# A fused attention, gated MLP and mixer kernel: four edits where its stages meet

## The chip, the core and the metric

The kernel runs on one core of one Trainium2 chip. The metric is the device time of one execution in microseconds; three runs of the kernel before took 915.26, 916.33 and 917.14 us, median 916.33.

## What is computed

Three layers in a row, for 4 batches of 448 tokens and 768 channels (12 heads of 64):

```
scores = q @ k.T / sqrt(64) - log(448);  x = sigmoid(scores) @ v           # attention
xk, xr = mu * x + (1 - mu) * x_prev                                        # mix with the token before
x = sigmoid(xr @ w_r) * (relu(xk @ w_k) ** 2 @ w_v)                        # gated MLP
h = relu(x.T @ w_tok1) @ w_tok2;   u = x + h.T                             # token mixing
out = u + relu(u @ w_ch1) @ w_ch2                                          # channel mixing
```

## The kernel before

Two batches lie beside one another as 896 columns, channels on partitions, so `rows` holds six rows of 128 channels by 896 columns. All stages run once for batches 0 and 1 and again for 2 and 3: `attention`, `first_part` (gated MLP and token mixing), `second_part` (channel mixing).

The large products keep about 22 bits of each operand: weight and activation are split into a high half (rounded to fp32r by ACT) and a low half (what is left, subtracted by DVE). `products` (line 293) multiplies high by high, high by low and low by high, for each tile of 128 in the sum, 512 and 384 columns wide one after the other (`WIDE`), so a channel product is 6 x 3 x 2 = 36 matmuls. The weights come as 8-byte numbers and are made into fp32 by the kernel: `w_raw` loads one on SP's queue, `w_form` takes two passes of ACT (lines 195, 196), `w_join` two of DVE (199, 202), `w_high` rounds on ACT (240), `w_low` subtracts on DVE (244). `raws`, formed weights and halves have three buffers each.

The order of work is written out by hand: each engine runs its instructions in the order of the program. `weights()` hands out the halves of the next weight and puts the steps for later weights into the list `due`; `products` takes one step from it (`tick`) after each tile of its sum, so the preparation of weights lies between matmuls. Four PSUM buffers of two banks go round (`new_ps`).

The places that matter:

- Start: the first loads of k and q go out on SP (lines 117, 118); twelve idle matmuls (`WARM`, line 132) run on zeros; then come the first scores (160), of 64 rows for each of two heads, evicted by a sigmoid on ACT (169).
- End of the gated MLP: line 382 multiplies a row by the product. Its rows are transposed for token mixing by `y_transpose` (319), whose result is evicted in two pieces: ACT 321, DVE 322 for three quarters, then ACT 323, DVE 324 for the tail.
- Token mixing, first product (lines 392 to 405): three pieces of two rows each, two halves `j` of eleven matmuls per piece. Row 5 is transposed after piece 0, `j` 0; only piece 2 reads it. All due steps of the first weight are run ahead of the pieces; those of the second lie in the second product.
- Token mixing, second product (lines 408 to 417): six rows `m`. A row takes 12 matmuls of 448 columns; then DVE adds it to `rows` (415), ACT rounds it to u's high half (416), DVE subtracts for the low half (417).
- Channel mixing: the first products read u row by row in the sum. The last products are added to `rows` (434) and written out as two transfers, one per batch, on SP (437).

Of the kernel before, what the change touches and what calls it, by code (L numbers as in the profile page):

```python
# [14 lines left out]
ALU = mybir.AluOpType  # L15
PSUM = bass.MemoryType.PSUM

B, H, S, D = 4, 12, 448, 64
# [4 lines left out]
P = 128  # L23
NT = C // P
# [2 lines left out]
W = 2 * S  # L27

WIDE = ((0, 512), (512, W - 512))
WARM = 12  # L30


def f32(ap):
    return ap.bitcast(F32)
# [3 lines left out]
def kernel(  # L38
# [17 lines left out]
    PE, ACT, DVE, POOL, SP = nc.tensor, nc.scalar, nc.vector, nc.gpsimd, nc.sync  # L56

    def pool(name, bufs, **kw):
        return ctx.enter_context(tc.tile_pool(name=name, bufs=bufs, **kw))

    const = pool("const", 1)
    wraw, wpool, wsplit = pool("wraw", 3), pool("wpool", 3), pool("wsplit", 3)
    tmps = pool("tmps", 2)
    psum = pool("psum", 4, space=PSUM)

# [10 lines left out]
    rows = const.tile([P, NT, W], F32, tag="rows", name="rows")  # L76
# [21 lines left out]
    def beside(ap):  # L98
        return ap.rearrange("p (b n) -> p b n", b=2)

    heads = [const.tile([P, 2 * 4 * P + S], F32, tag="qkv%d" % i, name="qkv") for i in range(3)]
    kns = [t[:, : 4 * P] for t in heads]
# [3 lines left out]
    def new_ps():  # L106
        return psum.tile([P, 1024], F32, tag="ps", name="ps")
# [7 lines left out]
    def load_kq(i):  # L115
        b, pr = units[i]
        SP.dma_start(out=kns[i % 3], in_=k[b * NPAIR + pr])
        SP.dma_start(out=qns[i % 3], in_=q[b * NPAIR + pr])

    def load_v(i):  # L120
        b, pr = units[i]
        SP.dma_start(out=vns[i % 3], in_=v[b * NPAIR + pr])

    warm = const.tile([P, 1], F32, tag="warm", name="warm")
    DVE.memset(warm, 0.0)
    ACT.activation(warm, warm, AF.Sigmoid)
# [4 lines left out]
    for _ in range(WARM):  # L131
        PE.matmul(idle[:, :S], zero[:, :P], zero, start=True, stop=True)  # L132

    load_kq(0)
    load_v(0)
    load_kq(1)
    load_v(1)
# [69 lines left out]
    for w in (w_r, w_k, w_v, w_tok1):  # L207
        n, r, cols = w.shape
# [14 lines left out]
    def w_raw(upto):  # L223
        for i, r, kt in step("raw", upto):
            raws[i] = wraw.tile([P, NT, P, 2], U32, tag="raw", name="raw")[:r, :kt]
            SP.dma_start(out=raws[i].rearrange("p t n e -> p (t n e)"), in_=seq[i][0])

    def w_form(upto):
        for i, r, kt in step("form", upto):
            forms[i] = wpool.tile([P, NT, P], F32, tag="wd", name="wd")[:r, :kt]  # L230
            narrow_1(forms[i].bitcast(U32), raws[i])

    def w_join(upto):
        for i, r, kt in step("join", upto):
            narrow_2(forms[i].bitcast(U32), raws.pop(i))

    def w_high(upto):
        for i, r, kt in step("high", upto):
            halves[i] = [wsplit.tile([P, NT, P], F32R, tag=n, name=n)[:r, :kt] for n in ("whi", "wlo")]
            ACT.copy(halves[i][0], forms[i])  # L240

    def w_low(upto):
        for i, r, kt in step("low", upto):
            DVE.tensor_tensor(out=halves[i][1], in0=forms.pop(i), in1=f32(halves[i][0]), op=ALU.subtract)  # L244
# [7 lines left out]
    def ahead(i):  # L252
        def low_form():
            w_low(i + 3)
            w_form(i + 4)

        def join_raw():
            w_join(i + 4)
            w_raw(i + 7)

        return [lambda: w_high(i + 3), low_form, lambda: None, join_raw]
# [31 lines left out]
    def products(ps, pieces, parts, at=0, count=None, hooks={}):  # L293
        count = count or len(parts)
        for i, (wh, wl, xh, xl) in enumerate(parts, at):
            passes = [(wh, xh), (wh, xl), (wl, xh)] if xl is not None else [(wh, xh), (wl, xh)]
            for n, (w, x) in enumerate(passes):
                for a, cols in pieces:
                    PE.matmul(  # L299
                        ps[:, a : a + cols],  # L300
                        w,
                        x[:, a : a + cols],
                        start=(i == 0 and n == 0),
                        stop=(i == count - 1 and n == len(passes) - 1),
                    )
            tick()
            if i in hooks:
                hooks[i]()

    def against(w, x, kt):  # L310
        return [(w[0][:, t], w[1][:, t], x[0][:, t], x[1][:, t]) for t in range(kt)]
# [41 lines left out]
    def first_part(b0):  # L353
        if b0 == 0:
            tok2_load()
        for m in range(NT):
            w = weights()
            ps = new_ps()
            products(ps, WIDE, against(w, xr, NT))
            ACT.activation(rows[:, m], ps[:, :W], AF.Sigmoid)  # L360
            if b0 == 0 and m < 3:
                tok2_stage(m)

        for m in range(F // P):
            w = weights()
            ps = new_ps()
            products(ps, WIDE, against(w, xk, NT))
            hi, lo = kk(m)
            t = tmps.tile([P, W], F32, tag="tmp", name="sq")
            ACT.activation(t, ps[:, :W], AF.Relu)  # L370
            DVE.tensor_tensor(out=t, in0=t, in1=t, op=ALU.mult)
            ACT.copy(hi, t)
            DVE.tensor_tensor(out=lo, in0=t, in1=f32(hi), op=ALU.subtract)

        for m in range(NT):
            ps = new_ps()
            for part in range(2):
                w = weights()
                parts = [(w[0][:, t], w[1][:, t], *kk(4 * part + t)) for t in range(4)]
                hooks = {2: lambda: y_transpose(m - 1)} if m and part == 0 else {}  # L380
                products(ps, WIDE, parts, 4 * part, 8, hooks)
            DVE.tensor_tensor(out=rows[:, m], in0=rows[:, m], in1=ps[:, :W], op=ALU.mult)  # L382

        wt1 = [weights()]
        held = due[:]
        due.clear()
        for f in held:
            f()
        i = use[0]
        use[0] += 1  # L390
        wt1.append(halves.pop(i))
        for piece in range(3):
            ps = new_ps()
            ms = slice(2 * piece, 2 * piece + 2)
            for j in range(2):
                wh, wl = wt1[j]
                x = [t[:, :, ms].rearrange("p r m b c -> p r (m b c)") for t in y]
                parts = [(wh[:, r], wl[:, r], x[0][:, r], x[1][:, r] if r < 3 else None) for r in range(4)]
                products(ps[:, j * 512 : (j + 1) * 512], ((0, 512),), parts)
                if piece == 0 and j == 0:  # L400
                    y_transpose(NT - 1)
            hi, lo = (t[:, :, ms].rearrange("p j m b c -> p j (m b c)") for t in h1)
            psv = ps.rearrange("p (j n) -> p j n", j=2)
            ACT.activation(hi, psv, AF.Relu)
            DVE.scalar_tensor_tensor(out=lo, in0=psv, scalar=0.0, in1=f32(hi), op0=ALU.max, op1=ALU.subtract)
        due[:] = ahead(i)

        for m in range(NT):
            ps = new_ps()
            for b in range(2):  # L410
                parts = [(h1[0][:, j, m, b], h1[1][:, j, m, b], wt2h[:, j], wt2l[:, j]) for j in range(2)]
                products(ps[:, b * 512 : b * 512 + S], ((0, S),), parts)
            hi, lo = (beside(p[:, m]) for p in u)
            r = beside(rows[:, m])
            DVE.tensor_tensor(out=r, in0=r, in1=banks(ps), op=ALU.add)  # L415
            ACT.copy(hi, r)  # L416
            DVE.tensor_tensor(out=lo, in0=r, in1=f32(hi), op=ALU.subtract)  # L417

    def second_part(b0):
        for half in range(2):  # L420
            for f in range(6):
                w = weights()
                ps = new_ps()
                products(ps, WIDE, against(w, u, NT))
                hi, lo = (p[:, f] for p in h2)
                ACT.activation(hi, ps[:, :W], AF.Relu)  # L426
                DVE.scalar_tensor_tensor(  # L427
                    out=lo, in0=ps[:, :W], scalar=0.0, in1=f32(hi), op0=ALU.max, op1=ALU.subtract
                )
            for m in range(NT):  # L430
                w = weights()
                ps = new_ps()
                products(ps, WIDE, against(w, h2, 6))
                DVE.tensor_tensor(out=rows[:, m], in0=rows[:, m], in1=ps[:, :W], op=ALU.add)  # L434
                if half:
                    for b in range(2):
                        SP.dma_start(
                            out=out[b0 + b, m * P : (m + 1) * P], in_=rows[:, m, b * S : (b + 1) * S]
                        )
                    if m == 3 and b0 + 2 < B:  # L440
                        for i in range(2):
                            load_kq((b0 + 2) * NPAIR + i)
                            load_v((b0 + 2) * NPAIR + i)
# [80 lines left out]
```

## Time and profile before

| what | us |
|---|---|
| median of three runs (lowest, highest) | 916.33 (915.26, 917.14) |
| the profiled execution, its own time | 914.43 |
| its span, first to last instruction | 912.7 |
| DVE busy in the span | 505.3 (55%) |
| ACT busy in the span | 420.0 (46%) |
| mean TensorE clock granted | 0.999 of full speed |

All times in the rows below are from the profiled execution. A row of the timeline gives start, duration, engine, line, operation, tile written and tiles read, shape and count; in brackets stands how long the engine was idle before and what ended that. A matmul's duration runs to its last result and overlaps the next one's, so the distance from start to start tells the pace. The chain of work shows what the end of the execution hangs on, merged to pieces: start, duration, engine, tile, line, count.

### The profile page before, as it was taken

To read this page: it belongs to the slowest core of one execution; us is meant where nothing else is said; L and a number is where in the kernel's file an instruction comes from. 1 tells how busy PE (TensorE), PEld (TensorE's weight loads), DVE (VectorE), ACT (ScalarE), POOL (GpSimd) and SP (SyncE) were. 2 spreads that over 40 slices of the span, in tenths; PEclk is the share of its full clock that TensorE was granted. 3 is DMA by queue.
4 is the path that set the end of the run, shared out by engine and by line. 5 is a ranking of instruction groups with operands and counts; after the bars stand their busy time and mean duration, and the time that the engine had idled before them with its cause. 6 is when DMAs were issued, how large, how long until landed. Compare 5 with 4: busy or idle time off the path is not lost.

```text
span 912.7 us, 10954 instructions
## 1 busy us (share of the span) xinstructions
PE 900.8 (99%) x4464; PEld 723.8 (79%) x4464; DVE 505.3 (55%) x563; ACT 420.0 (46%) x550; POOL 1.2 (0%) x9
## 2 busy tenths in 40 slices
PE   9999999999999999999999999999999999999997
PEld 3335888888887888888843468888988878888886
DVE  1776546656657555555535564465566575555551
ACT  5784645544434443343355644455444354334420
POOL 0000000000000000000000000000000000000000
PEclk9999999999999999999999999999999999999999
DMA  7542232223321333334654213222224123333311
GB/s 268 184 155 75 97 112 81 70 89 97 131 100 35 122 121 104 104 104 149 244 170 121 78 35 119 93 90 81 93 93 150 58 70 104 127 116 104 104 61 60
DMA packets 29426, 99.67 MB, mean 109 GB/s; under 512 B 3520, under 2 KB 9664, under 8 KB 29376
## 3 DMA queue, kind: packets, MB, share of 16 engines
q1 hardware_dynamic: 29376, 98.98, 32.7%
q8 instruction: 35, 0.57, 0.3%
q14 instruction: 15, 0.12, 0.0%
HBM read 93.46 MB, written 5.51 MB: 108 GB/s over the span
## 4 chain that ended last, share of the span: by engine, by line
PE 92%; DVE 5%; ACT 2%; issue 0%; POOL 0%; ACTq 0%; POOLq 0%
PE ps L299 74%; PE ps L160 8%; PE ps L176 8%; DVE two L417 1%; DVE rows L415 1%; ACT two L416 1%; PE ps L319 1%; DVE wd L199 1%; DVE wd L202 1%; PE ps L132 1%; ACT wd L195 0%; ACT raw L196 0%; DVE rows L382 0%; DVE two L322 0%; ACT whi L240 0%
## 5 line engine op out<-in xcount | busy, mean ns | idle before, releaser
L299 PE MATMUL ps<-one,whi 128*128 128x512 f32 (+1 forms) x1152 | 280.7, 365 | 0.0
L299 PE MATMUL ps<-two,whi 128*128 128x512 f32 (+1 forms) x1044 | 261.8, 367 | 4.1 <-ACT two L416 2.3
L299 PEld LDWEIGHTS ps<-one,whi 128*128 128x128 f32 x1152 | 208.1, 188 | 25.0 <-PE ps L176 0.7
L299 PEld LDWEIGHTS ps<-two,whi 128*128 128x128 f32 x1044 | 189.0, 188 | 30.3 <-ACT two L416 3.8
L299 PE MATMUL ps<-one,wlo 128*128 128x512 f32 x576 | 163.1, 364 | 0.0
L299 PE MATMUL ps<-two,wlo 128*128 128x512 f32 (+1 forms) x528 | 154.8, 367 | 0.0
L240 ACT CAST whi<-wd 128x768 fp32r<-128x768 f32 (+1 forms) x104 | 80.6, 775 | 138.4 <-PE ps L299 91.7
L244 DVE TENSOR_TENSOR wlo<-wd,whi 128x768 fp32r<-128x768 f32 (+1 forms) x104 | 91.6, 881 | 41.6 <-ACT whi L240 41.6
L299 PEld LDWEIGHTS ps<-one,wlo 128*128 128x128 f32 x576 | 104.4, 188 | 12.0
L199 DVE SCALAR_TENSOR_TENSOR wd<-wd,raw 128x768 uint32<-128x768 uint32 (+1 forms) x104 | 92.3, 887 | 30.5 <-ACT raw L196 27.9
L299 PEld LDWEIGHTS ps<-two,wlo 128*128 128x128 f32 x528 | 96.0, 188 | 12.2
L202 DVE SCALAR_TENSOR_TENSOR wd<-raw,wd 128x768 uint32<-128x768 uint32 (+1 forms) x104 | 92.2, 887 | 3.6
L169 ACT ACTIVATE rows<-ps 128x896 f32<-128x896 f32 x96 | 80.3, 924 | 21.5 <-PE ps L160 21.5
L195 ACT ACTIVATE wd<-raw 128x768 f32<-128x768 f32 (+1 forms) x104 | 88.1, 847 | 0.0
L196 ACT ACTIVATE raw<-raw 128x768 uint32<-128x768 uint32 (+1 forms) x104 | 86.6, 833 | 0.0
L160 PE MATMUL ps<-qkv 64*128 64x448 f32 x384 | 78.9, 550 | 0.0
L176 PE MATMUL ps<-rows,qkv 128*64 128x448 f32 x384 | 77.4, 545 | 0.0
L434 DVE TENSOR_TENSOR rows<-rows,ps 128x896 f32<-128x896 f32 x24 | 26.1, 1088 | 81.0 <-PE ps L299 81.0
L160 PEld LDWEIGHTS ps<-qkv 64*128 64x128 f32 x384 | 35.3, 188 | 42.8 <-issue 38.0
L176 PEld LDWEIGHTS ps<-rows,qkv 128*64 128x64 f32 x384 | 25.4, 136 | 49.1 <-issue 32.5
L426 ACT ACTIVATE one<-ps 128x896 fp32r<-128x896 f32 x24 | 22.0, 918 | 88.6 <-PE ps L299 88.6
L427 DVE SCALAR_TENSOR_TENSOR one<-ps,one 128x896 fp32r<-128x896 f32 x24 | 26.2, 1091 | 65.8 <-ACT one L426 65.8
(57 smaller groups left out, 443.6 us busy)
## 6 DMA issues: line engine op xcount, KB each, us to landing
raw<-in_moe_w_ch_dram SPq DMA_DIRECT2D x48, 768.0 KB, 4.1
raw<-in_moe_w_k_dram SPq DMA_DIRECT2D x16, 768.0 KB, 4.2
raw<-in_moe_w_v_dram SPq DMA_DIRECT2D x24, 512.0 KB, 3.6
raw<-in_moe_w_r_dram SPq DMA_DIRECT2D x12, 768.0 KB, 4.3
qkv<-in_k_dram SPq DMA_DIRECT2D x24, 256.0 KB, 2.8
qkv<-in_v_dram SPq DMA_DIRECT2D x24, 256.0 KB, 2.7
qkv<-in_q_dram SPq DMA_DIRECT2D x24, 224.0 KB, 3.0
out_dram<-rows SPq DMA_DIRECT2D x24, 224.0 KB, 2.2
```

What stands on the lines that cost most here:

```text
L160: PE.matmul(ps[:, h * 512 : h * 512 + S], kns[i % 3][me, c * P : (c + 1) * P], qns[i % 3][me], start=True, stop=True,)
L169: ACT.activation(a, banks(ps), AF.Sigmoid, bias=-math.log(S), scale=1.0 / math.sqrt(D))
L176: PE.matmul(ps[h * D : h * D + D, :S], vns[i % 3][:, h, c], att[c][:, h], start=(c == 0), stop=(c == 3))
L195: ACT.activation(f32(dst), f32(raw[..., 1]), AF.Copy, scale=2.0**-112)
L196: ACT.activation(raw[..., 0], raw[..., 0], AF.Copy, bias=0.4375, scale=0.875 * 2.0**-29)
L199: DVE.scalar_tensor_tensor(out=dst, in0=dst, scalar=3, in1=raw[..., 0], op0=ALU.logical_shift_left, op1=ALU.bitwise_or)
L202: DVE.scalar_tensor_tensor(out=dst, in0=raw[..., 1], scalar=0x80000000, in1=dst, op0=ALU.bitwise_and, op1=ALU.bitwise_or)
L240: ACT.copy(halves[i][0], forms[i])
L244: DVE.tensor_tensor(out=halves[i][1], in0=forms.pop(i), in1=f32(halves[i][0]), op=ALU.subtract)
L299: PE.matmul(ps[:, a : a + cols], w, x[:, a : a + cols], start=(i == 0 and n == 0), stop=(i == count - 1 and n == len(passes) - 1),)
L427: DVE.scalar_tensor_tensor(out=lo, in0=ps[:, :W], scalar=0.0, in1=f32(hi), op0=ALU.max, op1=ALU.subtract)
L434: DVE.tensor_tensor(out=rows[:, m], in0=rows[:, m], in1=ps[:, :W], op=ALU.add)
```

## The change

Four edits.

1. Token mixing: the subtraction for u's low half is issued one row later, after the next row's add; ACT's copy reads the row as one run of 896 columns. The due steps of both token weights now go into `due` together ahead of the pieces, so forms and joins lie in piece 0; the second weight's rounding and subtraction come after the pieces.
2. Row 5 is transposed after `j` 1 of piece 0, where it was after `j` 0.
3. Start: q's first load goes out on ACT's queue, k's in two pieces (128 columns, then 384) on SP, all ahead of the idle matmuls, of which there are nine for twelve. The pool of formed weights has two buffers for three.
4. The very last product is done by columns: 512 columns, their add and the first batch's output on SP, then 384 columns, their add and the second batch's output on ACT.

```diff
-WARM = 12
+WARM = 9
...
-    wraw, wpool, wsplit = pool("wraw", 3), pool("wpool", 3), pool("wsplit", 3)
+    wraw, wpool, wsplit = pool("wraw", 3), pool("wpool", 2), pool("wsplit", 3)
...
+    ACT.dma_start(out=qns[0], in_=q[0])
+    SP.dma_start(out=kns[0][:, :P], in_=k[0][:, :P])
+    SP.dma_start(out=kns[0][:, P:], in_=k[0][:, P:])
     warm = const.tile([P, 1], F32, tag="warm", name="warm")
...
-    load_kq(0)
     load_v(0)
...
         wt1 = [weights()]
-        held = due[:]
-        due.clear()
-        for f in held:
-            f()
         i = use[0]
         use[0] += 1
         wt1.append(halves.pop(i))
+        due.extend([lambda: w_form(i + 4), lambda: None, lambda: w_join(i + 4), lambda: w_raw(i + 7)])
...
-                if piece == 0 and j == 0:
+                if piece == 0 and j == 1:
                     y_transpose(NT - 1)
...
-        due[:] = ahead(i)
+        due.extend([lambda: w_high(i + 3), lambda: w_low(i + 3)])
+
+        def u_low(m):
+            DVE.tensor_tensor(out=u[1][:, m], in0=rows[:, m], in1=f32(u[0][:, m]), op=ALU.subtract)
...
-            hi, lo = (beside(p[:, m]) for p in u)
             r = beside(rows[:, m])
             DVE.tensor_tensor(out=r, in0=r, in1=banks(ps), op=ALU.add)
-            ACT.copy(hi, r)
-            DVE.tensor_tensor(out=lo, in0=r, in1=f32(hi), op=ALU.subtract)
+            ACT.copy(u[0][:, m], rows[:, m])
+            if m:
+                u_low(m - 1)
+        u_low(NT - 1)
...
+                if half and b0 + 2 == B and m == NT - 1:
+                    for b, queue in ((0, SP), (1, ACT)):
+                        at, cols = WIDE[b]
+                        products(ps, (WIDE[b],), against(w, h2, 6))
+                        r = rows[:, m, at : at + cols]
+                        DVE.tensor_tensor(out=r, in0=r, in1=ps[:, at : at + cols], op=ALU.add)
+                        queue.dma_start(
+                            out=out[b0 + b, m * P : (m + 1) * P], in_=rows[:, m, b * S : (b + 1) * S]
+                        )
+                    continue
```

## Rows read from the trace of the kernel before

**Rows 1.** The page: busy time of the engines.
```profile
PE 900.8 (99%) x4464; PEld 723.8 (79%) x4464; DVE 505.3 (55%) x563; ACT 420.0 (46%) x550; POOL 1.2 (0%) x9
```
**Rows 2.** TensorE's waits: line, for whom, us in total, times, longest.
```profile
PE ps L299 <- ACT two L416: 2.3, 4, 0.9
PE ps L299 <- DVE two L417: 1.8, 4, 0.5
PE ps L319 <- DVE rows L382: 1.7, 2, 0.9
```
**Rows 3.** Timeline, TensorE: token mixing's second product, then channel mixing's first and second.
```profile
264.46 0.37 PE L299 MATMUL ps<-wt2h,one 128*128 128x448 f32 x1
...
279.18 0.98 PE L299 MATMUL ps<-two,whi 128*128 128x512 f32 x4
...
289.61 0.97 PE L299 MATMUL ps<-two,whi 128*128 128x512 f32 x4
```
**Rows 4.** The chain of work, merged: two stretches of matmuls.
```profile
251.80 12.84 PE ps L299 x55
...
288.69 168.33 PE ps L299 x832
```
**Rows 5.** Timeline, DVE and ACT: rows of token mixing's second product, first and last.
```profile
269.04 0.96 DVE L202 SCALAR_TENSOR_TENSOR wd<-raw,wd 128x768 uint32<-128x768 uint32 x1
...
269.91 1.08 DVE L415 TENSOR_TENSOR rows<-rows,ps 128x896 f32<-128x896 f32 x1
...
271.03 0.94 ACT L416 CAST two<-rows 128x896 fp32r<-128x896 f32 x1 [3.02 <-DVE rows L415]
...
272.00 1.09 DVE L417 TENSOR_TENSOR two<-rows,two 128x896 fp32r<-128x896 f32 x1 [1.01 <-ACT two L416]
...
287.55 1.09 DVE L417 TENSOR_TENSOR two<-rows,two 128x896 fp32r<-128x896 f32 x1 [1.00 <-ACT two L416]
```
**Rows 6.** Timeline, TensorE: around the transposes of row 5.
```profile
249.45 0.40 PE L299 MATMUL ps<-two,wlo 128*128 128x512 f32 x1
...
250.71 1.09 PE L319 MATMUL ps<-ident,rows 128*128 128x128 f32 x8 [0.86 <-DVE rows L382]
...
251.56 0.71 PE L299 MATMUL ps<-two,whi 128*128 128x512 f32 x2
```
**Rows 7.** Timeline, DVE and ACT at the same place.
```profile
249.57 1.08 DVE L382 TENSOR_TENSOR rows<-rows,ps 128x896 f32<-128x896 f32 x1
...
251.31 0.89 ACT L196 ACTIVATE raw<-raw 128x768 uint32<-128x768 uint32 x1
...
254.10 0.95 DVE L322 TENSOR_TENSOR two<-ps,two 128x768 fp32r<-128x768 f32 x1
...
255.48 0.42 DVE L324 TENSOR_TENSOR two<-ps,two 64x256 fp32r<-64x256 f32 x1 [0.43 <-ACT two L323]
```
**Rows 8.** Start: the idle matmuls (timeline), line 160's durations, ns min/median/max.
```profile
1.26 4.66 PE L132 MATMUL ps<-rows 128*128 128x448 bf16 x12 [1.26 <-POOL rows L129]
...
L160 PE MATMUL ps<-qkv x16: 536/536/846, 5.8 to 8.8; 64*128 64x448 f32 x16
```
**Rows 9.** First q load: its issue (timeline), KB and us to landing (DMA view).
```profile
1.17 0.42 SPq L118 DMA_DIRECT2D qkv<-in_q_dram  x1
...
qkv<-in_q_dram SPq DMA_DIRECT2D x1, 224.0 KB, 2.8
```
**Rows 10.** End: the last add and outputs (timeline), and their landing (DMA view).
```profile
907.91 1.09 DVE L434 TENSOR_TENSOR rows<-rows,ps 128x896 f32<-128x896 f32 x1 [6.18 <-PE ps L299]
909.02 0.81 SPq L437 DMA_DIRECT2D out_dram<-rows  x2
...
out_dram<-rows SPq DMA_DIRECT2D x2, 224.0 KB, 2.1
```
**Rows 11.** Groups by line: a DVE operation of 448 columns; busy us, mean ns.
```profile
L290 DVE TENSOR_TENSOR wt2l<-rows,wt2h 128x448 fp32r<-128x448 f32 x2 | 1.2, 622 | 2.5 <-ACT wt2h L289 2.5
```
**Rows 12.** Second attention: us, busy by engine, TensorE's granted clock, DMA share, GB/s.
```profile
457.00:533.00 76.00, 76.00 (x385) 30.24 (x384) 36.21 (x41) 46.02 (x59) 0.00 (x0) 1.00 0.35 108
```

## The prediction, made before the changed kernel was run

> **What bounds the kernel now.** I read the page's busy times first. TensorE is busy 900.8 us of a span of 912.7 us [rows 1], so no more than 11.9 us can go without taking matmuls away, and the question is where those 11.9 us lie. The list of who TensorE waited for answers most of it: four waits each on lines 416 and 417, the rounding copy and the subtraction that make u, and two on line 382 [rows 2]. The chip runs the middle stages twice, once for each pair of batches, so each pass has two waits of each u kind and one on line 382. The rest is the start and the end.
>
> Then I went to the places. After token mixing the first channel product starts at 279.18 us and the second at 289.61 us [rows 3]: 10.43 us for a product of 36 matmuls. In the undisturbed stretch that follows, 832 matmuls take 168.33 us [rows 4], so 0.2023 us each and 7.28 us for 36. The product loses **3.15 us**. This is more than the waits listed there, because each wait also restarts the matmul pipeline. The second pass has the same picture at 730 us.
>
> Why is u late? Per row DVE adds (1.08 us), ACT rounds (0.94), DVE subtracts (1.09), and DVE can't take the next row's add while it waits for ACT: the add at 269.91, the copy at 271.03, the subtraction at 272.00 and its end at 273.09 make 3.1 us per row, with the next add a little ahead of that end [rows 5]. TensorE makes a row in 72 matmuls / 6: from 264.46 to 279.18 [rows 3] is 14.72 / 6 = 2.45 us. Also the chain starts late: row 0's products are done near 264.46 + 2.45 + 0.2 = 267.1, but DVE is still in a weight join until 270.00 [rows 5]. The last subtraction, at 287.55, ends at 288.64 [rows 5], nine tenths of the way through the first channel product.
>
> The other seam: the last row's transposes stand after eleven matmuls of token mixing. The last of these starts at 249.45 and the next matmul would follow 12.84 / 55 = 0.2335 us later [rows 4], at 249.68; the transposes start at 250.71 [rows 6]. **1.02 us** are lost. They wait for the product at line 382, 249.57 to 250.65 [rows 7], which was itself late behind a join.
>
> **The change part by part.** *u's subtraction one row behind.* Nothing is added or removed: the six adds, copies and subtractions stay, but DVE now has the add of row m ahead of the subtraction of row m-1, whose copy is done by then. DVE's cost per row is then 1.08 + 1.09 = 2.17 us, ACT's 0.94 [rows 5], both below TensorE's 2.45. Beside it the form and join of a weight move from the row stage to the first token product, so only a rounding and a 0.96 us subtraction stand ahead of row 0. Row 5's products end near the start of the first channel product plus 0.2, and add, copy (or the subtraction of row 4 beside it) and the last subtraction follow: 1.08 + 1.09 + 1.09 = 3.3 us later u is whole. The product needs row 5 only after five sixths of its 7.28 us, at 6.1 us. So the whole 3.15 us goes, with 2.6 us to spare: 2 x 3.15 = **6.3 us**. What is late next is nothing up to that slack. The two halves of this edit back one another: staggering alone, with the old start at 269.91, would end near 269.91 + 6 x 2.17 + 1.09 = 284.0, still ahead of the need at 285.3.
>
> *Transposes after twenty-two matmuls.* The eleven moved ahead take 11 x 0.2335 = 2.57 us, so the transposes come up at 249.68 + 2.57 = 252.25, 1.6 us after line 382 ends. Gain 2 x 1.02 = **2.0 us**. This has a price to look at: the transposes' evictions now stand on ACT and DVE behind one more weight (ACT two passes, DVE two). From the rows: ACT's first form ends at 252.20 [rows 7], two more passes of 0.9 at most end at 254.0; DVE then joins, 2 x 0.96 [rows 5], until about 256.0, and the evictions that ran on DVE from 254.10 to 255.90 [rows 7] end near 257.9, the large one near 257.0. The third token product, which alone reads them, starts at 252.25 + 0.85 + 5.14 = 258.2 (the eight transposes as from 250.71 to 251.56 [rows 6], 22 matmuls). Slack 1.2 us for the large eviction, and the small one is read only nine matmuls in. So the order costs nothing, but this is the thinnest cover in the change; past it each us late costs 2 us in all. The added form needs its raw weight, asked for one weight earlier as always; SP has only these loads then. The next raw load is issued some 14 us sooner with nothing behind it.
>
> *Two formed-weight buffers for three.* A form now reuses the buffer whose subtraction stood before it on DVE, in the steady loop by a whole product of 7.28 us. At the seam that subtraction follows line 382 and ends near 251.6, and the form would start near 252.2: 0.6 us of cover, 0.96 per pass if it were gone, inside the slack above. I take nothing.
>
> *Start.* Twelve idle matmuls run from 1.26 for 4.66 us, and the first scores come at 5.8 [rows 8]. The first q load lands 2.8 us after its issue at 1.17 [rows 9], at 4.0, so scores wait for the idle matmuls, not for data. A matmul of 448 columns every 0.373 us (448 / 1.2, 12 of them 4.5 of the 4.66) is the 1.2 GHz level; three fewer bring the scores to 5.85 - 1.12 = 4.73. q goes ahead of ACT's work, k in two pieces on SP, the second at q's old place, 1.17; the same bytes land by about 4.0, leaving 0.7 us. ACT's issue, 0.42 if it is like SP's [rows 9], delays a table load that nobody needs before the first scores. SP's later loads keep their places, since one issue is added and one leaves. But the clock limits the gain. Among the sixteen first scores the longest took 846 ns and the median 536 [rows 8]: the first pair still ran at the lower level, and the rise came just after 5.85. If the rise stays at its time, the 1.12 us gained are run at half speed and only 0.56 is kept; if the clock were up by 4.73, 1.12. A rise later by x takes x / 2 off, below nothing from 1.1 us on. I take **0.6**, nearest to the row.
>
> The Trainium skill ("TensorE: Matmul & The Clock Gate", Part 1) says that the warm-up is an amount of time, not of matmuls, and that its moment varies from run to run; by that this term is 0.56 in a run like this one, against 1.12 by the count of matmuls. No run of before can tell the two apart.
>
> *End.* The last add takes 1.087 us for 896 columns from 907.91, two output issues follow at 909.02, 0.81 us together, and land in 2.1 [rows 10]. After: TensorE does 18 matmuls of 512 columns, then 18 of 384. At 0.2335 for 512 and 0.175 for 384 (0.2045 for 448 [rows 3], less the same step) they take 7.36, 0.08 more; at most 0.3 more if the narrow ones go no faster than 0.19. The first add and output lie under the second piece. The second add has 384 columns: with 622 ns for 448 [rows 11] and 1.04 ns a column, 0.556, which is 0.53 less. The second issue, 0.38 later, falls away. Sum 0.53 + 0.38 - 0.08, and 0.1 for a lone transfer: **0.9**. An output issue on ACT is not in the trace; SP's is the nearest row. Bounds: 1.2, and 0.1 if the second piece waits for the add that reads the same PSUM tile or the ACT issue is dear.
>
> **Sum:** 6.3 + 2.0 + 0.6 + 0.9 = 9.8 us. The profiled execution took 914.43 us (span 912.7, 1.7 around it), so its counterpart would take 904.6. The median of the runs shown is 916.33, 1.9 above it, with a spread of 1.9; taking the same off the median gives **906.5 us**.
>
> **Rivals.** *The small terms fail* (0.13): start and end give nothing, or cost a little, because the clock rises late or the last product's second half waits. Seams alone: 916.33 - 8.3 = 908.0; with the start 1 us worse, 909.0. For it: the start's first pair at the lower level, and an ACT output never seen. Against it: 0.7 us of cover for the loads, and a last add that is shorter by its columns.
>
> *The wait moves to the third token product* (0.07): the transposes' evictions, behind a second form and join, come late. At 1.5 us past the slack per pass this gives back 3 us: 909.5. For it: DVE's row of joins just there. Against it: the 1.2 us of slack worked out above.
>
> *The edit doesn't reach the path* (0.05): u's lag shows in TensorE's waits on line 417 as before, because something else, such as an add waiting for a PSUM tile, keeps DVE at 3.1 us per row. Then 6.3 us stay: 912.8, or within 0.2% if the small terms fail too. Against it: the wait of DVE before each subtraction is on the copy of its own row, 1.01 us [rows 5].
>
> *Slower* (0.03): the lower clock level lasts into attention. The shorter run of idle matmuls leaves 64-row scores to bring the clock up; every us at 1.2 GHz costs 0.5. The other terms and a full 1.12 make 10.3 us, so it decides from 20.6 us of such running on; it is 0.2% slower (918.2) at 24.3 us. For it: the rise came only once scores had begun. Against it: the second attention holds the full level for all its 76 us with these same matmuls [rows 12].
>
> **How the numbers follow.** The forecast has 0.72. A measurement of this kernel can tell about 0.2%, 1.8 us, from no change. Faster: the forecast, the first two rivals and some of the third, 0.93. Same: 0.04, slower 0.03. The range goes from 903.8 (the start at 1.1, the end at 1.2, and a median as low as the profiled counterpart) to 909.5, which takes in the small terms failing and the moved wait at the price given.
>
> **What would show it.** The list of TensorE's waits should have neither line 416, 417 nor 382 before it; the first channel product should take 7.3 us; the subtractions should stand 2.45 us apart; the transposes should follow the second run of eleven matmuls without a gap; the scores should start near 4.7 with about three pairs at over 800 ns; the last add should take 0.56 us with one output issue after it. A wait of the third token product on line 322, a score stretch that stays long, or a gap between the last product's halves would make it wrong.

## The result, and the profile of the changed kernel

| | before | after |
|---|---|---|
| median, same chip, us | 916.74 (915.26 to 917.67) | 904.69 (904.53 to 905.27) |
| profiled execution, us | 914.43 | 905.27 |
| its span, us | 912.7 | 903.5 |
| after / before | | 0.9874 (95%: 0.9858 to 0.9890) |

The change takes 12.05 us off the median and 9.2 us off the profiled execution. The two differ, and that is the most instructive part of this case: before's profiled execution was 0.8 us below the lowest of its timed ones, while after's is the longest of its own.

The page of after, its busy row. It answers to [rows 1]: TensorE is busy 2.9 us less and the span is 9.2 us shorter.

```profile
PE 897.9 (99%) x4461; PEld 723.9 (80%) x4461; DVE 505.4 (56%) x564; ACT 420.1 (46%) x550; POOL 1.2 (0%) x9
```

The list of TensorE's waits (line, for whom: us in total, times, longest) answers to [rows 2]. All three kinds named there are gone. What is left is the start, and a new wait of 0.8 us on line 441, the split add of the last product.

```profile
PE ps L135 <- POOL rows L132: 1.3, 1, 1.3
PE ps L301 <- DVE rows L441: 0.8, 1, 0.8
```

The timeline of TensorE at the two seams (start, length, line, operation, count). The transposes now follow the 22nd matmul at once, where [rows 6] had a hole of 1.02 us, and the first channel product goes from 277.64 to the second's first row at 284.93: 7.29 us, where [rows 3] had 10.43.

```profile
251.55 0.39 PE L301 MATMUL ps<-two,wlo 128*128 128x512 f32 x1
251.78 1.04 PE L321 MATMUL ps<-ident,rows 128*128 128x128 f32 x8
...
277.64 0.98 PE L301 MATMUL ps<-two,whi 128*128 128x512 f32 x4
...
284.93 0.97 PE L301 MATMUL ps<-two,whi 128*128 128x512 f32 x4
```

The timeline of DVE in the same stretch (the bracket is the idle time before it and what ended it). The transposes' evictions (lines 324, 326) come at 255.47 and 256.85; line 416 adds a row and line 408 subtracts the one before. Against [rows 5] the subtraction no longer waits for a copy: it follows the add without idle time, the add waits for TensorE, and the subtractions stand 2.45 us apart.

```profile
255.47 0.95 DVE L324 TENSOR_TENSOR two<-ps,two 128x768 fp32r<-128x768 f32 x1
...
256.85 0.42 DVE L326 TENSOR_TENSOR two<-ps,two 64x256 fp32r<-64x256 f32 x1 [0.43 <-ACT two L325]
...
268.03 1.09 DVE L416 TENSOR_TENSOR rows<-rows,ps 128x896 f32<-128x896 f32 x1 [0.76 <-PE ps L301]
269.04 1.08 DVE L408 TENSOR_TENSOR two<-rows,two 128x896 fp32r<-128x896 f32 x1
270.49 1.09 DVE L416 TENSOR_TENSOR rows<-rows,ps 128x896 f32<-128x896 f32 x1 [0.36 <-PE ps L301]
271.49 1.08 DVE L408 TENSOR_TENSOR two<-rows,two 128x896 fp32r<-128x896 f32 x1
```

The chain of work at the start (start, length, count): nine idle matmuls, the first scores, the second unit's scores. The first scores come 1.12 us sooner than in [rows 8] and take 0.9 us longer than the second ones.

```profile
1.26 3.54 PE ps L135 x9
4.80 4.07 PE ps L162 x16
...
12.02 3.21 PE ps L162 x16
```

The end: the timeline of TensorE, DVE and ACT's queue, and the landing of the last output (DMA view: KB, us).

```profile
891.57 1.09 DVE L447 TENSOR_TENSOR rows<-rows,ps 128x896 f32<-128x896 f32 x1 [6.19 <-PE ps L301]
...
895.33 0.39 PE L301 MATMUL ps<-one,wlo 128*128 128x512 f32 x1
895.75 0.69 DVE L441 TENSOR_TENSOR rows<-rows,ps 128x512 f32<-128x512 f32 x1 [3.10 <-PE ps L301]
896.50 0.61 PE L301 MATMUL ps<-one,whi 128*128 128x384 f32 x2 [0.78 <-DVE rows L441]
...
899.93 0.55 DVE L441 TENSOR_TENSOR rows<-rows,ps 128x384 f32<-128x384 f32 x1 [3.48 <-PE ps L301]
900.51 0.35 ACTq L442 DMA_DIRECT2D out_dram<-rows  x1
...
out_dram<-rows ACTq DMA_DIRECT2D x1, 224.0 KB, 2.0
```

The last add is as short as forecast (0.55) and only one output issue follows it. But the second piece of the product waits until the first piece's add has read the same PSUM tile: its first matmul stands at 896.50, 1.17 us after the last one of the first piece, where about 0.25 is usual, so some 0.92 us are lost. From the previous row's add to the end of the span it is 11.9 us, against 12.1 before: the end gave about 0.1.

So the 9.2 us of the profiled pair are 0.47 at the start (second scores at 12.02 against 12.49), 4.22 in the first pass, 4.38 in the second, and 0.1 at the end. In the second pass the first channel product gives 3.14 (from 10.42 to 7.28) and the transposes 1.03, as in the first; the other 0.2 us lie in that pass's gated MLP, away from the seams, where two of the stretches between transposes took 9.7 us for 9.8.

### The profile page after: what moved, and what is told of

Read it like the earlier page. It is cut to its first block, busy times and chain, and to the rows that moved or that the text cites. A ratio compares the mean times of both kernels' runs of the same rounds, so it can differ in the third digit from the quotient of the medians.

```text
span 903.5 us, 10939 instructions
## 1 busy us (share of the span) xinstructions
PE 897.9 (99%) x4461; PEld 723.9 (80%) x4461; DVE 505.4 (56%) x564; ACT 420.1 (46%) x550; POOL 1.2 (0%) x9
## 4 chain that ended last, share of the span: by engine, by line
PE 99%; DVE 0%; POOL 0%; issue 0%; POOLq 0%
PE ps L301 81%; PE ps L162 9%; PE ps L178 8%; PE ps L321 1%; PE ps L135 0%; DVE rows L441 0%; POOL rows L132 0%; POOLq L523 0%
## 5 line engine op out<-in xcount | busy, mean ns | idle before, releaser
L301 PE MATMUL ps<-one,whi 128*128 128x384 f32 (+1 forms) x1152 | 281.6, 365 | 0.8 <-DVE rows L441 0.8
L301 PE MATMUL ps<-one,wlo 128*128 128x512 f32 (+1 forms) x576 | 164.0, 364 | 0.0
L301 PEld LDWEIGHTS ps<-one,wlo 128*128 128x128 f32 x576 | 104.4, 188 | 12.1
```

Source lines behind the costliest of these rows:

```text
L301: PE.matmul(ps[:, a : a + cols], w, x[:, a : a + cols], start=(i == 0 and n == 0), stop=(i == count - 1 and n == len(passes) - 1),)
```

## Experiments

Each kernel but before_again is the changed one with the edit shown. Medians stand beside runs of the kernel before on the same chip, whose medians were 916.03, 915.63 and 915.10 us in the three groups of runs. A ratio is to that median, with its 95% interval. After itself was timed only in the first comparison (before at 916.74), so a difference to its 904.69 also holds what the groups differ by, up to 1.6 us.

**u as before** (u_undone): subtraction in its own row, and the old places of the weight's steps.

```diff
+        held = due[:]
+        due.clear()
+        for f in held:
+            f()
...
-        due.extend([lambda: w_form(i + 4), lambda: None, lambda: w_join(i + 4), lambda: w_raw(i + 7)])
...
-        due.extend([lambda: w_high(i + 3), lambda: w_low(i + 3)])
+        due[:] = ahead(i)
...
-            if m:
-                u_low(m - 1)
-        u_low(NT - 1)
+            u_low(m)
```

> The changed kernel with its first edit taken back whole: u's subtraction in its own row, and the due steps of the token weights where they were before. Theory 1 (the gain is the sum of the waits that the trace of before shows): the two seams come back with 2 x 3.15 us, so the median goes from 904.7 to 911.0 us, a ratio to the kernel before of 0.993 to 0.994, and TensorE waits on the rounding copy and on the subtraction, four times each, 4 us in all. Rival (the medians moved by 12.05 us and the profiled executions by 9.2 only; the missing 2.9 us belong to these seams, as a cost that shows in some executions and not in the profiled one): the median goes to 913 us or more, and single executions lie 2 us apart again.

Measured: 913.63 us (912.61 to 915.21), ratio 0.9975 (0.9966 to 0.9984). That is 8.9 us more than after, the rival's time, where the waits and their restarts alone account for 6.3 (2 x 3.15). The profile (span 912.0, 8.5 above after) shows where the rest is in that execution: seven of the eight waits for u in [rows 2] are back, and behind them the granted clock of TensorE falls. The first fence has the waits, TensorE's timeline and a row of the chain of u_undone, the second stretches of it (us: length, busy time and count of PE, PEld, DVE, ACT, POOL, granted clock, DMA share, GB/s).

```profile
PE ps L301 <- ACT two L420: 2.3, 4, 0.9
PE ps L301 <- DVE two L411: 1.1, 3, 0.5
...
283.92 0.68 PE L301 MATMUL ps<-two,whi 128*128 128x512 f32 x2 [0.45 <-DVE two L411]
...
285.89 0.91 PE L301 MATMUL ps<-two,whi 128*128 128x512 f32 x2 [0.88 <-ACT two L420]
287.01 1.12 PE L301 MATMUL ps<-two,whi 128*128 128x512 f32 x2 [0.22 <-DVE two L411]
...
287.01 169.50 PE ps L301 x832
```
```profile
282.75:286.16 3.41, 2.04 (x7) 1.23 (x8) 2.38 (x3) 1.26 (x2) 0.00 (x0) 1.00 0.00 0
286.17:289.57 3.40, 3.18 (x9) 2.28 (x9) 2.98 (x4) 2.67 (x4) 0.00 (x0) 0.50 0.00 0
...
736.73:740.13 3.40, 3.25 (x8) 2.35 (x9) 2.87 (x3) 2.69 (x5) 0.00 (x0) 0.50 0.00 0
```

In the first stretch TensorE works 2.04 of 3.41 us between waits; right behind it the clock is at 0.50 (1.2 GHz, the lower level) for 3.4 us, and a pair of matmuls takes 1.12 us where it took 0.68. This happens in both passes. The 832 matmuls that start at 287.01 take 169.50 us, against 168.33 for the same ones in [rows 4]: 1.2 us; in the second pass it is 1.0 (166.25 for the 165.26 of u_serial, below). With 6.3 for the waits that makes up the 8.5 us of the span. So the waits for u cost more than their length in this execution, by a mechanism that before's first profile did not show: the same waits stand there at an undisturbed clock.

**The subtraction alone back in its own row** (u_serial), and **the weight's steps alone back** (u_old_dues): the two halves of the u edit.

```diff
-            if m:
-                u_low(m - 1)
-        u_low(NT - 1)
+            u_low(m)
```

> The changed kernel with u's subtraction back in its own row; the due steps stay in the first token product. Theory 1: the late start is gone, so the serial chain of 3.1 us per row begins near 266.2 us and the subtraction of row 5 ends near 266.2 + 6 x 3.1 = 284.8 us, where the first channel product (from 277.6 us) needs that half at 284.1 us. Only about 0.7 us per pass come back, 906.1 us in all, nearly all of them on row 5's subtraction. Rival (the lag of DVE behind ACT is what costs, wherever the chain starts): most of 2 x 3.15 us comes back, 909 to 911 us.

```diff
+        held = due[:]
+        due.clear()
+        for f in held:
+            f()
...
-        due.extend([lambda: w_form(i + 4), lambda: None, lambda: w_join(i + 4), lambda: w_raw(i + 7)])
...
-        due.extend([lambda: w_high(i + 3), lambda: w_low(i + 3)])
+        due[:] = ahead(i)
```

> The changed kernel with the due steps of the token weights where they were before (a form and a join ahead of row 0's add); the subtraction stays one row behind. Theory 1: the chain starts 1.5 to 3 us late, catches up at 2.17 us per row against TensorE's 2.45, and is done by 284 us less the 1.5 us that the start and the transposes save, ahead of the need: 904.7 us, no wait for u. The transposes' evictions stand behind one weight less. Rival (the late start is what costs): 2 to 3 us per pass come back, 909 to 911 us.

u_serial: 908.35 us (906.94 to 909.0), ratio 0.9920 (0.9907 to 0.9934). u_old_dues: 905.2 us (904.4 to 905.43), ratio 0.9887 (0.9873 to 0.9900), no wait for u, as its theory had it. The wait of TensorE that u_serial has, twice:

```profile
PE ps L301 <- DVE two L408: 0.9, 2, 0.5
```

With the subtraction in its own row, the first channel product of u_serial took 8.25 us (277.37 to 285.62) against 7.28, 1.9 us for both passes; with the subtraction a row behind, the old place of the join costs nothing that can be measured. Staggering alone is enough; moving the weight's steps alone covers 2.2 of the same 3.15 us per pass. By the median u_serial (3.7 us above after) is nearer its rival than its theory; by the trace it is the theory, with the one wait on row 5's subtraction, 1.9 us in both passes for a forecast 1.4. Its profile, the quickest of its four executions, also had a slower matmul pace in the first long stretch (below), 0.8 us; the rest of its median is not explained.

**The transposes after eleven matmuls again** (transposes_early):

```diff
-                if piece == 0 and j == 1:
+                if piece == 0 and j == 0:
```

> The changed kernel with row 5's transposes back after the first eleven matmuls. Theory 1: TensorE waits twice for the product at the end of the gated MLP, as before, 1.02 us each at the pace of its matmuls: 904.7 + 2.0 = 906.7 us. Rival (the moved due steps already lie between, so that the gap is filled by another order, or the later transposes had cost something of their own): 904.7 to 905.5 us.

Measured: 907.1 us (906.29 to 907.66), ratio 0.9911 (0.9896 to 0.9926): 2.4 us above after by medians, where the theory had 2.0. By the profiles it is 1.0 in span, with a start that was 0.9 sooner, so 1.9. The hole is back in its place, twice:

```profile
PE ps L321 <- DVE rows L384: 1.7, 2, 0.8
...
249.12 1.09 PE L321 MATMUL ps<-ident,rows 128*128 128x128 f32 x8 [0.83 <-DVE rows L384]
```

**The last product** whole again (end_old), and by columns with a PSUM tile of its own for the second piece (end_own_psum):

```diff
-                if half and b0 + 2 == B and m == NT - 1:
-                    for b, queue in ((0, SP), (1, ACT)):
...
-                    continue
```

> The changed kernel with the last product, its add and its outputs as they were before. Theory (the wait between the halves eats the 0.9 us that the shorter add and the single last output issue give): 904.6 to 904.8 us, no difference to be seen. Rival (the halves gain as forecast): 905.6 us.

```diff
                     for b, queue in ((0, SP), (1, ACT)):
                         at, cols = WIDE[b]
+                        if b:
+                            ps = new_ps()
```

> The changed kernel, with a PSUM buffer of its own for the second half of the last product. Theory: the 0.92 us gap between the halves is TensorE waiting for the add that reads the first half in the same PSUM tile; it goes, and so do 0.9 us: 903.8 us, no wait on the line of that add. Rival (the gap has another cause, such as a restart that any change of piece brings): 904.7 us and the gap stays.

end_own_psum: 903.61 us (903.16 to 904.55), ratio 0.9865 (0.9850 to 0.9880), the quickest kernel of this case. Its timeline of DVE and TensorE at the end:

```profile
890.87 1.09 DVE L449 TENSOR_TENSOR rows<-rows,ps 128x896 f32<-128x896 f32 x1 [6.19 <-PE ps L301]
...
894.63 0.40 PE L301 MATMUL ps<-one,wlo 128*128 128x512 f32 x1
894.87 0.51 PE L301 MATMUL ps<-one,whi 128*128 128x384 f32 x2
...
898.25 0.56 DVE L443 TENSOR_TENSOR rows<-rows,ps 128x384 f32<-128x384 f32 x1 [2.50 <-PE ps L301]
```

The second piece now starts 0.24 us after the first piece's last matmul, and the end of the span comes 10.9 us after the previous row's add, 1.0 less than in after. That the hole was the shared tile's is shown by this edit: nothing else changed.

end_old: 905.7 us (905.11 to 906.58), ratio 0.9887 (0.9872 to 0.9903), the rival's figure, 1.0 above after where the profiles of before and after had differed by 0.1 at the end. In end_old's profile the two outputs landed in 2.8 us, not 2.1, with an instruction fetch in flight beside them (DMA view: KB, landing; the queue of the fetch):

```profile
out_dram<-rows SPq DMA_DIRECT2D x2, 224.0 KB, 2.8
...
q14 instruction: 1, 0.01, 0.3%
```

From the previous row's add to the end of the span end_old took 12.8 us, of which the longer landing is 0.7; before took 12.1 and before_again (below) 12.0, both with a landing of 2.1. Whether the end edit as written is worth 0.1 us or 1.0 stays open: these two timelines against after's 11.9 say 0.1, the medians of end_old and after say 1.0 with ranges of about 1 us, and which landing time is usual for two outputs was not settled.

**Twelve idle matmuls and the old loads** (start_old), and **seven** with the end of end_own_psum (end_own_warm7):

```diff
-WARM = 9
+WARM = 12
...
-    ACT.dma_start(out=qns[0], in_=q[0])
-    SP.dma_start(out=kns[0][:, :P], in_=k[0][:, :P])
-    SP.dma_start(out=kns[0][:, P:], in_=k[0][:, P:])
...
+    load_kq(0)
```

> The changed kernel with the start as before: twelve idle matmuls and the first loads of k and q on SP. Theory (scores begin 1.12 us later, and by how much of that the end moves depends on when the clock rises: half of it if the rise comes later than the scores' begin in both, all of it if earlier): 905.2 to 905.8 us. Rival (the rise moves with the number of matmuls, so nothing was gained): 904.7 us.

```diff
-WARM = 9
+WARM = 7
...
+                        if b:
+                            ps = new_ps()
```

> The changed kernel with a PSUM buffer of its own for the second half of the last product, and seven idle matmuls for nine. Theory: scores begin 0.75 us sooner, near 3.98 us, when the data has just come, and half to all of that is kept: 903.6 - 0.4 to 0.75 = 902.9 to 903.2 us. Rival (the first loads now set the begin, or the clock rises later for it): 903.6 us or more.

start_old: 905.98 us (904.7 to 906.0), ratio 0.9883 (0.9868 to 0.9899). end_own_warm7: 903.56 us (903.38 to 904.49), ratio 0.9871 (0.9851 to 0.9892), the same as with nine. The chain at the start of end_own_warm7, then of end_own_psum:

```profile
4.05 4.12 PE ps L162 x16
...
11.33 3.21 PE ps L162 x16
```
```profile
4.80 3.37 PE ps L162 x16
...
11.32 3.21 PE ps L162 x16
```

Two idle matmuls fewer bring the first scores 0.75 us sooner, and these then take 4.12 us in place of 3.37: the second unit starts at the same time. The traces say why. The record of the granted clock begins in each of them with the rise to the upper level: at 5.86 us in end_own_warm7 and at 5.09 in end_own_psum, at 6.30 in before and at 6.50 in after. Until then matmuls run at half speed: in after a pair of the first scores starts every 0.74 us ahead of the rise and every 0.37 behind it. (The views count the time ahead of the first record as 1.00.) So a rise one us later moves all that follows by half of that. With half the rise's time taken off the start of the second unit's scores, the profiles fall into three groups:

| idle matmuls | profiles | the clock's rise, us | second unit's scores start, us | that start less half the rise |
|---|---|---|---|---|
| 12 | 3 | 5.00 to 6.30 | 11.90 to 12.49 | 9.34 to 9.40 |
| 9 | 10 | 4.17 to 7.24 | 10.92 to 12.39 | 8.77 to 8.84 |
| 7 | 1 | 5.86 | 11.33 | 8.40 |

So three idle matmuls fewer are worth some 0.57 us and two fewer some 0.37, about half of the 1.12 and 0.75 us by which the scores come sooner. In one execution the moment of the rise moves the end by more than that: it lay anywhere from 4.17 to 7.24 us with the same nine matmuls, and a rise 0.77 later hides the gain of seven in the pair above. Medians that spread over 1 us don't settle gains of this size: end_own_warm7's is the rival's time, and start_old's excess of 1.3 us over after, the high end of its theory, need not be the start. In start_old's profile the second scores start 0.12 sooner than in after; its span is 0.7 longer by a slower pace of the matmuls in the first long stretch, 116.10 us for the 115.34 of after (the rows are from its chain):

```profile
11.90 3.21 PE ps L160 x16
...
81.91 116.10 PE ps L299 x570
```

Whether the number of idle matmuls moves the rise at all can't be told from three profiles and one; these lie within the spread of the ten. This agrees with the Trainium skill ("TensorE: Matmul & The Clock Gate", Part 1), which counts the warm-up in time and says that its moment varies.

**Is it the clock that u's waits cost beside their length?** u_undone_filled is u_undone with ten matmuls per pass put into the waits, 512 columns each, whose product nobody reads; u_undone_filled_2 is the same kernel again, and u_undone_full_fill has seventeen. fill(n) puts n of them behind a tile of the sum (`hooks`) or behind the first third of its matmuls (`mids`). before_again is the kernel before, profiled once more.

```diff
+                    spare = new_ps()
+                    def fill(n):
+                        for _ in range(n):
+                            PE.matmul(spare[:, :512], w[0][:, 0], u[0][:, 0, :512], start=True, stop=True)
+                    hooks = {3: lambda: fill(2), 4: lambda: fill(4)}
+                    mids = {4: lambda: fill(2), 5: lambda: fill(2)}
```

> As the run with the first edit taken back, but TensorE has ten matmuls of 512 columns with nobody reading them (2.3 us at its pace) in the first channel product of each pass, laid where it waits for u's rows 4 and 5. u comes as late as there; only the waiting is filled with work. Theory (in many executions the waits also bring the granted clock down to half for some us right behind them, as in the profiled execution of the run before: 0.5 for 3.4 us in each pass): the clock stays up, the waits themselves stay, so 904.7 + 6.3 = 911.0 us, up to 911.6 for matmuls that don't fit a wait, and the executions lie within about 1 us. Rival (the 2.6 us beyond the waits have another source): 913.6 us or more, spread over 2.6 us as there.

> The filled run once more, for one look at one execution: five of its nine took 913.8 to 914.3 us, four 911.2 to 911.6, and the profiled one was of the lower group. If this one is of the upper group, theory: a stretch at half the granted clock near 285 us or 735 us or both; rival: no such stretch, and the time lies in the pace of the matmuls over long stretches (0.2034 us each for 0.2021) or at the start.

```diff
-                    hooks = {3: lambda: fill(2), 4: lambda: fill(4)}
-                    mids = {4: lambda: fill(2), 5: lambda: fill(2)}
+                    hooks = {3: lambda: fill(3), 4: lambda: fill(6)}
+                    mids = {4: lambda: fill(4), 5: lambda: fill(4)}
```

> As the filled run, with seventeen unread matmuls per pass, more than the waits can hold, so that TensorE never stands still in the first channel product. They take 17 x 0.2335 = 4.0 us per pass in place of the waits' 3.15. Theory (executions that take about 2.6 us more are executions in which the clock falls behind the waits, and the fill of the run before left enough of them for that): one group of times, 904.7 + 7.9 = 912.6 us, within about 1.2 us. Rival (the 2.6 us have nothing to do with standing still): two groups again, near 912.6 and 915.2 us.

> The kernel before once more, for one look at another execution: the profiled one of before took 914.4 us, while the medians of its runs are 915.6 to 916.7. Theory: in an execution of 915.5 us or more the granted clock falls to half behind the waits for u, in one pass or both, some 1.2 us each. Rival: such an execution shows no fall, and the time lies elsewhere.

u_undone_filled: 913.83 us (911.22 to 914.25), ratio 0.9970 (0.9955 to 0.9984), in two groups: four executions of 911.22 to 911.55 and five of 913.83 to 914.25, none between: the lower is the theory's time, the upper the rival's. Its profile is of the lower group (911.46), with no wait for u and no fall of the clock; u_undone_filled_2, 914.5, is of the upper, again with a clock of 1.00 throughout. u_undone_full_fill: 913.06 us (912.25 to 914.64), ratio 0.9972 (0.9959 to 0.9986), no fall either. before_again: 916.98 us. The long stretches of matmuls in the chain of u_undone_filled and then u_undone_filled_2:

```profile
82.15 115.34 PE ps L301 x570
287.06 168.32 PE ps L301 x832
531.76 115.33 PE ps L301 x570
736.66 165.25 PE ps L301 x814
```
```profile
81.06 116.11 PE ps L301 x570
286.94 169.43 PE ps L301 x832
532.75 116.11 PE ps L301 x570
738.63 166.32 PE ps L301 x814
```

The two profiles of one kernel differ by a pace: each of the four stretches is 0.7% longer in the second, +0.77, +1.11, +0.78 and +1.07, together 3.7 us, less a start that was 1.1 sooner. The clock is granted in full in both. That shows what sets these two executions apart, one each and on two chips; that the two groups of timed ones differ by the pace too is likely, not shown, and why a stretch has one pace or the other is open.

before_again's stretches about the same place, and two rows of its chain:

```profile
285.40:288.82 3.42, 1.81 (x7) 0.95 (x6) 2.42 (x3) 1.92 (x3) 0.00 (x0) 1.00 0.00 0
288.83:292.24 3.41, 3.23 (x9) 2.84 (x10) 2.97 (x5) 2.31 (x4) 0.00 (x0) 0.50 0.00 0
...
82.17 116.11 PE ps L299 x570
...
289.01 169.81 PE ps L299 x832
```

Here the kernel before has both: the clock at 0.50 behind the waits of the first pass, by which the 832 matmuls take 1.48 us more than in [rows 4], and none in the second pass; and the slower pace in two stretches, 0.76 each. With its start 0.34 sooner that is 2.7 us, for the 2.5 by which its span exceeds that of the first profile, with nearly the same list of waits.

So, as far as shown: the fall of the clock comes right behind the u waits (three times in six passes with these waits in the profiles, and nowhere in the eleven profiles without them or with matmuls in them, u_serial's with its one wait of 0.5 us per pass among these), and it costs 1.0 to 1.5 us each time. Not shown: how often it comes in timed executions. By its medians no filled kernel is clearly quicker than u_undone; the lower group of u_undone_filled is, by 1.0 us against u_undone's quickest, and its upper group is the slower pace where it was profiled. In u_undone_full_fill, with ten of twelve executions in 912.25 to 913.61 and two near 914.6, the two were not separated.

## Why the prediction was right, point by point, and where it was not

| term | forecast, us | first pair of profiles | that edit alone undone, median less 904.69 |
|---|---|---|---|
| u a row behind | 6.3 | 6.3 | 8.9 |
| transposes later | 2.0 | 2.1 | 2.4 |
| start | 0.6 | 0.47 | 1.3 |
| end | 0.9 | 0.1 | 1.0 |
| gated MLP of the second pass | 0 | 0.2 | |
| sum | 9.8 | 9.2 | 13.6 |

The passes gave 4.22 + 4.38 = 8.6: 3.15 for u and 1.07 for the transposes in the first, 3.14, 1.03 and the 0.2 of the gated MLP in the second. The last column's sum is more than the whole gain of 12.05: each of its terms carries the spread of two medians, about 1 us, and what the groups of runs differ by. Taken by the ratios, each against before in its own group, the column reads 9.3, 3.4, 0.8 and 1.2. The two small terms lie inside this scatter and rest on the traces.

**u** went as worked out: the product took 7.29 us for a forecast 7.28, the subtractions stood 2.45 us apart, DVE waited for TensorE and no longer for ACT, u was whole at 281.04, 3.4 us into the product for a forecast 3.5, and the two halves of the edit covered one another, the staggering wholly and the moved steps in part. What the term left out is that the waits cost clock as well in some executions.

**The transposes** stood without a gap, and their thinnest cover held: the large eviction ended at 256.42 and the small one at 257.27 [the DVE rows of after], for a forecast of near 257.0 and 257.9, which become 256.5 and 257.4 with the 0.47 us of the start taken off. No wait of the third token product appeared, so that rival fell.

**The start** was sized right, and for the reason given: a rise that stays at its time leaves half of the 1.12 us, 0.56. After's rise came 0.20 us later than before's (6.50 against 6.30), which takes off 0.10 by the prediction's own rule, and 0.47 was measured. Between the three profiles with twelve idle matmuls and the ten with nine, the rise's moment taken out, the term is 0.57. That this pair's rises lay so close is luck: among profiles with nine idle matmuls they differ by up to 3 us, and half of that is more than the term itself. The price of the new loads was none: no score waited for them. They were not tried apart from the number of idle matmuls, nor the two formed-weight buffers by themselves; no form of ACT waits for a buffer in after's list of waits.

**The end** is the term of the sum that was mis-sized: 0.9 forecast, about 0.1 in the trace. The forecast had its parts right (the add 0.55 for 0.556, one issue fewer) and named the case that came, "if the second piece waits for the add that reads the same PSUM tile", as the lower bound 0.1, but chose the upper side. The wait of 0.92 us ate the gain; end_own_psum, which takes it away, brought 1.1 us by medians and 1.0 by the trace, so that its end is 1.1 us shorter than before's, inside the forecast's bounds.

**The step to the median** failed in the other direction. "Taking the same off the median" assumed that the 1.9 us between before's profiled execution and its median have nothing to do with the change. The profiled counterpart was forecast at 904.6 and came at 905.27, off by 0.7, in the main the end's 0.8; the median was forecast at 906.5 and came at 904.69. After's median lies 0.6 below its profiled execution, not 1.9 above. before_again shows what such slower executions of before hold: 1.48 us of clock behind the u waits, which the change removes with the waits, and 1.5 us of pace, which also appears in kernels with the new seams. How the 1.8 us by which the median came out lower than forecast divide among these two and mere scatter (before's median was 915.10 to 916.74 in four groups) is not settled. The end's error and this one partly cancel in the median; either alone would have stayed inside the range, since the two seams, 8.4 of the 9.2 us, came as sized. The range of 903.8 to 909.5 held the result, and faster it was.

**The rivals.** The moved wait and the unreached path are refuted by the rows of after; the small terms failed in part (the end); no lower clock lasted into attention, as the second unit's scores took 3.21 us.

## What to carry to other kernels

Where one engine adds and then subtracts what another engine rounds in between, put the subtraction one row behind: that alone removed all waits for u here. When a product is cut so that its first part can be read early, give the parts PSUM tiles of their own, or the reader holds up the second part. Price a wait from more than one profiled execution before taking a difference to the median: the same waits left the clock alone in one execution and halved it for 3.4 us in the next.

## What the runs showed of the hardware that was not expected

- Four waits of 0.9 us and less in one product were in three of six passes followed by 3.4 us at half the granted clock (0.50), at a cost of 1.0 to 1.5 us; the same kernel showed it in one pass and not in the other.
- The moment at which the granted clock first rises lay between 4.17 and 7.24 us in ten profiles with the same nine idle matmuls, and the matmuls that follow move by half of that.
- At a granted clock of 1.00 the same 570 matmuls take 115.34 or 116.11 us, and 832 take 168.32 or 169.43: two paces, each held over a whole stretch. The slower one came in the first long stretch of five of the kernels' profiles (before_again, start_old, u_serial, u_undone_filled_2, u_undone_full_fill) and in later stretches of two. Its cause is open.
- The other bank of a PSUM tile that DVE was reading was not written meanwhile, as this program orders it: 0.92 us, gone with a second tile. Whether the chip or the program's ordering by tiles demands that wait was not tried.
- An output issued from ACT took 0.35 us to issue and 2.0 us to land, about the same as from SP (0.41 each and 2.1 in before).
